# Where two columns of ones are filled: ahead of all loads, or behind the loads of chunk 2

## The chip, the cores and the metric

The kernel runs on one core of a Trainium2 chip. The metric is the device time of one execution in microseconds (us), median of three runs. A profile of one execution lies beside it; its rows count from the start of the profiled span.

## The reference

Two blocks follow one another. First comes a causal attention with 4 batches, 8 heads, 768 positions and 64 values per head. Heads 0, 2 and 6 see every earlier position ("retrieval"); the other five see the first 4 positions and a window of the last 64 ("streaming"). Its output, laid out as 3072 rows of 512, goes through two matrix products with a leaky ReLU between them:

```python
scores = scale * np.matmul(q, k.transpose(0, 1, 3, 2))
mask = np.where(retr[0, :, 0, 0, None, None], full_mask, stream_mask)
scores = np.where(mask[None, :, :, :], scores, -1000000000.0)
a = np.exp(scores - max)
a = a / (np.sum(a, axis=-1, keepdims=True) + 1e-09)
attn_out = np.matmul(a, v)
...
h = x @ w_in                    # 512 -> 2048
g = np.maximum(0.01 * h, h)
out = g @ w_out                 # 2048 -> 512
```

## The kernel before

The positions are cut into eight chunks of 384: chunks 0 and 1 are batch 0, chunks 2 and 3 batch 1, and so on. Each chunk goes through three stages: attention (class `Attention`, one unit for each streaming head and two to five for each retrieval head), the first product (`in_slots`, 16 ticks of four matmuls, L420) and the second product (`out_slots`, L433). TensorE (PE) does the scores (L302, L337, L282 for the first four positions, the "sinks"), the products with V (L271) and both MLP products. ScalarE (ACT) does the exponentials and the leaky ReLU, VectorE (DVE) the masks (L310, L312, L346), the division by the sum (L368, L370) and the copies out of the second product (L438).

The sum of a row of the softmax comes out of the product with V: each head's V has 65 columns, and the last is 1.0. V lies in two buffers, `va[0]` for the even batches and `va[1]` for the odd ones, each `[128, 6 blocks, 8 heads, 65]`. A load of V (`load_v`, L104) writes columns 0 to 63 of the three blocks of its chunk; column 64 is filled once per buffer, by a memset in `zero_small` (L159). `vb` holds the same V shifted by 64 positions, for the windows, and is copied out of `va` by `v_shift` (L132, L133). `zero_small` also zeroes `ksink` and `vs`, and `zero_keys` (L153, L154) zeroes the halves of the key buffer `kt` that no head fills.

The order is written by hand (`manual_schedule`): each engine takes its instructions in the order of the program, and a wait at one holds all behind it on that engine. The program text is, with the calls that matter here:

```python
zero_small(0, nc.vector)        # L476: va[0]'s ones
...
load_v(0, ...); load_qk(1); load_v(1)
load_in(...); load_out(...)     # both MLP matrices
load_qk(2)
load_v(2)                       # L498: into va[1], blocks 0 to 2
...                             # attention of chunk 0
zero_small(1, nc.vector)        # L555: va[1]'s ones
nc.vector.tensor_copy(vs[1][0:32, :, D], m_sink[0:32, :])
a1 = Attention(1, xt_eng="v").slots()
```

Loads from memory go through GpSimd's queue (POOL; `load_qk` L99, `load_v` L104, `load_in` L121, `load_out` L125). SyncE's queue (SP) carries the transposing copies of q and k (`turn_dma`, L210: `qb` to `qd` and `kb` to `kd`), `v_shift`, and the writes of the output (L439). Chunks 0 and 1 are transposed on TensorE, chunks 2 to 7 by those transposing copies; from `kd` DVE spreads the keys of each head into `kt` (`spreads`, L219).

After the attention of chunk 0 the order is: attention of chunk 1 mixed with the first product of chunk 0; the first product of chunk 1; seven slots (22 matmuls) of the second product of chunk 0; `spreads(2)`; the attention of chunk 2 mixed with what is left of the second products of chunks 0 and 1 and with `spreads(3)`; and then a loop over chunks 2 to 7 in which attention, first product and second product of neighbouring chunks are mixed slot by slot.

The buffers `kb` and `qb` are doubled: `load_qk(4)` waits for the transposing copies of chunk 2. `va[1]` takes chunks 2 and 3, then 6 and 7.

Of the kernel before, what the change touches and what calls it, by code (L numbers as in the profile page):

```python
# [21 lines left out]
def kernel(  # L22
# [12 lines left out]
    nc = tc.nc  # L35
    B, H, S, D = q.shape
# [21 lines left out]
    def bf(name, *shape):  # L58
        return one.tile([128, *shape], BF16, name=name)
# [14 lines left out]
    va = [bf(f"va{i}", 6, H, D + 1) for i in range(2)]  # L74
# [81 lines left out]
    def zero_small(i, eng):  # L156
        eng.memset(ksink[i][:], 0.0)
        eng.memset(vs[i][:], 0.0)
        eng.memset(va[i][:, :, :, D], 1.0)  # L159


    qx = {}
# [311 lines left out]
    load_sinks(0)  # L474
    zero_keys(0, nc.vector)
    zero_small(0, nc.vector)  # L476
    nc.vector.memset(shift[:], 0.0)
    for a in ats:
        nc.vector.memset(a[:, :, 1:3, :], 0.0)
    nc.gpsimd.memset(m_caus[:], 1.0)  # L480
# [72 lines left out]
    v_shift(1)  # L553
    zero_keys(1, nc.vector)
    zero_small(1, nc.vector)  # L555
    nc.vector.tensor_copy(vs[1][0:32, :, D], m_sink[0:32, :])

# [73 lines left out]
```

## Time and profile before

| | |
|---|---|
| device time, median of 3 | 276.74 us (276.65 to 277.5) |
| profiled execution, its own time | 275.88 us |
| its span (first to last instruction) | 274.2 us |
| mean granted TensorE clock | 0.944 of full speed |
| busy: PE, ACT, DVE, POOL | 229.7, 140.3, 95.5, 71.5 us |
| PE's share of the span | 84% |

The span is what the rows divide up; the 1.68 us between it and the execution's own time lie outside all rows. Busy shares are averages over the whole span, so a stretch in which an engine stands still is found in the slices and in the timelines. "Idle before" is the time that an engine stood still just ahead of an instruction, with the instruction or transfer that ended it.

### The profile page before, as it was taken

The page shows a single profiled execution, that of the slowest core. Times are in us where ns is not written, and L with a number is a line of the kernel's source. Part 1 is how long each engine was busy: PE and PEld are TensorE (multiplying, and loading weights), DVE is VectorE, ACT ScalarE, POOL GpSimd, SP SyncE. Part 2 cuts the span into 40 slices and gives each one's busy share as a digit, 9 for nine tenths or more (in the row PEclk, how much of TensorE's full clock was granted, in tenths as well). Part 3 has the DMA queues.
Part 4 walks back from the last instruction along what each step waited for, and adds up shares of the span by engine and source line. Part 5 has one row for each costly group of instructions (what it writes and reads, how often), then busy time and mean ns, then how long its engine had stood idle before and what let it go on. Part 6 is the DMA issues. An engine that isn't in the chain of part 4 may idle for free.

```text
span 274.2 us, 5026 instructions
## 1 busy us (share of the span) xinstructions
PE 229.7 (84%) x2036; PEld 138.0 (50%) x2036; DVE 95.5 (35%) x272; ACT 140.3 (51%) x305; POOL 71.5 (26%) x94
## 2 busy tenths in 40 slices
PE   1785000198999989999999999999999999999995
PEld 1463000066555555665565566656665566655544
DVE  7867100125200673265235315522353124311012
ACT  2859000067674455767565576565645766633300
POOL 8995135734700000399000007500000000000000
PEclk9979655589999999999999999999999999999999
DMA  7999999999990114599951088908210101010022
GB/s 82 131 138 201 214 206 166 148 126 165 190 105 2 44 54 108 107 146 155 185 153 39 2 186 89 167 7 175 75 41 4 37 38 41 0 41 38 38 79 77
DMA packets 98167, 27.40 MB, mean 100 GB/s; under 512 B 90464, under 2 KB 93792, under 8 KB 98144
## 3 DMA queue, kind: packets, MB, share of 16 engines
q0 software_dynamic: 74448, 13.64, 66.0%
q1 hardware_dynamic: 23696, 13.44, 21.1%
q8 instruction: 16, 0.26, 0.4%
q14 instruction: 7, 0.06, 0.1%
HBM read 27.30 MB, written 6.29 MB: 123 GB/s over the span
## 4 chain that ended last, share of the span: by engine, by line
PE 76%; DMA 11%; POOL 8%; DVE 2%; issue 1%; ACT 1%; DVEq 0%; POOLq 0%
PE ph L420 30%; PE py L433 27%; DMA w_out_bf<-in_moe_w_out_dram 8%; PE po L271 6%; PE psS L302 5%; PE psS L433 3%; DMA va<-in_v_dram 3%; POOL va L104 2%; PE psS L337 2%; PE psS L376 2%; PE psS L282 2%; POOL qb L99 1%; POOL kb L99 1%; DVE xs L370 1%; POOL w_in_bf L121 1%
## 5 line engine op out<-in xcount | busy, mean ns | idle before, releaser
L420 PE MATMUL ph<-xt,w_in_bf 128*128 128x384 bf16 x512 | 102.0, 327 | 0.0
L433 PE MATMUL py<-w_out_bf,g 128*128 128x512 bf16 (+1 forms) x352 | 91.4, 374 | 0.0
L422 ACT ACTIVATE g<-ph 128x384 bf16<-128x384 f32 x128 | 62.9, 491 | 54.7 <-PE ph L420 54.1
L420 PEld LDWEIGHTS <-w_in_bf 128*128 128x128 bf16 x512 | 46.0, 98 | 30.5 <-issue 1.9
L433 PEld LDWEIGHTS <-g 128*128 128x128 bf16 x400 | 35.8, 98 | 26.2
L307 ACT ACTIVATE at<-psS 128x384 bf16<-128x384 f32 x81 | 39.2, 489 | 14.0 <-PE psS L302 12.8
L271 PE MATMUL po<-va,at 128*128 128x65 bf16 x246 | 21.0, 196 | 27.2 <-DVE at L312 27.2
L271 PEld LDWEIGHTS <-at 128*128 128x128 bf16 x252 | 16.3, 100 | 33.1 <-DVE at L312 27.4
L438 DVE COPY o<-py 128x512 f32<-128x512 f32 (+1 forms) x22 | 14.9, 677 | 44.6 <-PE py L433 44.5
L104 POOL DMA_DIRECT2D va<-in_v_dram x24 | 21.4, 916 | 5.2 <-DMA w_out_bf<-in_moe_w_out_dram 3.4
L114 POOL TENSOR_TENSOR vs<-vsf,m_sink 32x448 bf16<-32x448 f32 x3 | 2.8, 941 | 75.6 <-PE psS L302 40.5
L99 POOL DMA_DIRECT2D kb<-in_k_dram x21 | 18.8, 905 | 13.8 <-DMA kd<-kb 8.6
L346 DVE TENSOR_TENSOR ats<-ats,m_win 128x384 bf16<-128x384 bf16 x40 | 14.3, 358 | 21.9 <-ACT ats L342 21.5
L302 PE MATMUL psS<-qd,kt 128*128 128x384 bf16 (+2 forms) x81 | 20.7, 290 | 0.2 <-ACT at L307 0.2
L342 ACT ACTIVATE ats<-psS 128x384 bf16<-128x384 f32 x38 | 18.4, 488 | 4.5 <-PE psS L337 4.5
L99 POOL DMA_DIRECT2D qb<-in_q_dram x21 | 18.5, 904 | 7.1 <-DMA w_in_bf<-in_moe_w_in_dram 3.8
L285 ACT ACTIVATE at_sink<-psS 128x384 bf16<-128x384 f32 (+1 forms) x7 | 3.1, 445 | 30.4 <-PE psS L282 30.3
L312 DVE TENSOR_TENSOR at<-at,m_caus 128x128 bf16<-128x128 bf16 x24 | 5.6, 232 | 33.1 <-ACT at L307 33.0
L370 DVE TENSOR_TENSOR xs<-po,linv 128x384 bf16<-128x384 f32 x30 | 16.7, 557 | 1.0
L378 ACT ACTIVATE xt<-psS 128x384 bf16<-128x384 bf16 x24 | 11.7, 489 | 7.9 <-PE psS L376 7.6
L302 PEld LDWEIGHTS <-kt 128*128 128x128 bf16 x108 | 10.4, 99 | 9.6 <-issue 3.2
L337 PEld LDWEIGHTS <-kt 128*128 128x128 bf16 x240 | 12.3, 99 | 5.6 <-issue 0.2
(89 smaller groups left out, 195.0 us busy)
## 6 DMA issues: line engine op xcount, KB each, us to landing
out_dram<-o SPq DMA_DIRECT2D x23, 256.0 KB, 2.2
va<-in_v_dram POOLq DMA_DIRECT2D x24, 128.0 KB, 6.1
kb<-in_k_dram POOLq DMA_DIRECT2D x21, 128.0 KB, 5.9
qb<-in_q_dram POOLq DMA_DIRECT2D x21, 128.0 KB, 5.9
w_out_bf<-in_moe_w_out_dram POOLq DMA_DIRECT2D x4, 512.0 KB, 19.6
vb<-va SPq DMA_DIRECT2D x8, 195.0 KB, 3.1
w_in_bf<-in_moe_w_in_dram POOLq DMA_DIRECT2D x2, 512.0 KB, 9.6
w_in_bf<-in_moe_w_in_dram POOLq DMA_DIRECT2D x1, 1024.0 KB, 15.2
```

The lines of the kernel that those rows point to most:

```text
L99: nc.gpsimd.dma_start(out=t[:, g], in_=nat[nm][b, c, :, :, g])
L104: nc.gpsimd.dma_start(out=va[b % 2][:, 3 * c + g, :, 0:D], in_=nat["v"][b, c, :, :, g])
L271: nc.tensor.matmul(o, lhsT=lhsT, rhs=rhs, start=first, stop=False, skip_group_check=True)
L302: nc.tensor.matmul(s[:, off : off + w], lhsT=kt[i][:, p, hh, 128 * kj : 128 * kj + 128], rhs=q_of(n, p, lo, CH), start=(j == 0), stop=(j = ...
L307: nc.scalar.activation(out=a[:, 0:off], in_=s[:, 0:off], func=ACTF.Exp, scale=SM)
L337: nc.tensor.matmul(s[:, 64 * m : 64 * m + 64], lhsT=kt[i][:, p, hh, k0 : k0 + 128], rhs=q_of(n, p, 64 * m, 64 * m + 64), start=(m == 0), s ...
L342: nc.scalar.activation(out=av_, in_=s[:, 0:CH].rearrange("p (j e f) -> p j e f", j=3, e=2), func=ACTF.Exp, scale=SM)
L370: nc.vector.tensor_tensor(xs[:], po[:, :, :, 0:D], linv.to_broadcast([128, 3, 2, D]), op=ALU.mult)
L420: nc.tensor.matmul(ph[:, 0:CH], lhsT=w_in_bf[:, g, 128 * t : 128 * t + 128], rhs=xts[n][:, g, :], start=(g == 0), stop=(g == KG - 1))
L422: nc.scalar.activation(out=gs[n][:, t, :], in_=ph[:, 0:CH], func=ACTF.Prelu, alpha=0.01)
L433: nc.tensor.matmul(py[n][:, 0 : c1 - c0], lhsT=gs[n][:, ng, 128 * tt : 128 * tt + 128], rhs=w_out_bf[:, ng, c0:c1], start=(ng == 0), stop= ...
L438: nc.vector.tensor_copy(o[:, 0 : c1 - c0], py[n][:, 0 : c1 - c0])
```

## The change

The memset of V's ones leaves `zero_small`, which is called once for each buffer (L476, L555). Both buffers are filled at the beginning instead, on the same engine, behind the memset of `shift` and ahead of those of `ats`; in the text of the program this stands ahead of every load of V.

```diff
     def zero_small(i, eng):
         eng.memset(ksink[i][:], 0.0)
         eng.memset(vs[i][:], 0.0)
-        eng.memset(va[i][:, :, :, D], 1.0)
...
     zero_small(0, nc.vector)
     nc.vector.memset(shift[:], 0.0)
+    for i in range(2):
+        nc.vector.memset(va[i][:, :, :, D], 1.0)
     for a in ats:
         nc.vector.memset(a[:, :, 1:3, :], 0.0)
```

## Rows read from the trace of the kernel before

**Rows 1.** Page, the span in 40 slices of 6.86 us: tenths busy, granted clock.

```profile
PE   1785000198999989999999999999999999999995
PEclk9979655589999999999999999999999999999999
```

**Rows 2.** Waits of 0 to 100 us: in total, times, longest.

```profile
PE po L271 <- DVE at L312: 27.2, 1, 27.2
POOL va L104 <- DVE va L159: 1.4, 1, 1.4
```

**Rows 3.** Timeline of DVE, 0 to 54 us: start, duration, instruction, idle before.

```profile
5.19 0.10 DVE L159 MEMSET va<- 128x48 bf16 x1
...
27.77 0.49 DVE L158 MEMSET vs<- 128x520 bf16 x1
53.09 0.10 DVE L159 MEMSET va<- 128x48 bf16 x1 [24.82 <-DMA va<-in_v_dram]
53.33 0.17 DVE L556 COPY vs<-m_sink 32x8 bf16<-32x8 bf16 x1
```

**Rows 4.** Chain that ended last, pieces of 0 to 110 us: start, us, what.

```profile
21.84 22.38 DMA w_out_bf<-in_moe_w_out_dram
...
45.79 6.97 DMA va<-in_v_dram
...
54.02 1.28 PE psS L282 x4
...
71.45 14.53 PE ph L420 x84
85.98 4.75 PE py L433 x22
```

**Rows 5.** Timeline of POOL, 0 to 75 us: issues of loads, their duration, idle before.

```profile
5.58 0.90 POOL L104 DMA_DIRECT2D va<-in_v_dram  x1
...
14.81 2.68 POOL L104 DMA_DIRECT2D va<-in_v_dram  x3
...
34.34 0.88 POOL L99 DMA_DIRECT2D qb<-in_q_dram  x1 [3.77 <-DMA w_in_bf<-in_moe_w_in_dram]
...
65.64 2.70 POOL L99 DMA_DIRECT2D kb<-in_k_dram  x3 [8.56 <-DMA kd<-kb]
```

**Rows 6.** PE's windows of 1 us: length, busy (instructions), granted clock, DMA share, GB/s.

```profile
29.00:30.00 1.00, 0.00 (x0) 1.00 1.17 219
30.00:31.00 1.00, 0.00 (x0) 0.58 1.09 207
...
56.00:57.00 1.00, 1.00 (x7) 0.50 3.19 164
```

**Rows 7.** Timeline of SP's queue, 20 to 110 us: issues of transfers.

```profile
52.30 4.43 SPq L210 DMA_TRANSPOSE kd<-kb  x1
...
65.27 3.59 SPq L210 DMA_TRANSPOSE kd<-kb  x1
...
69.59 0.54 SPq L133 DMA_DIRECT2D vb<-va  x1
```

**Rows 8.** Tile `kd`, the issue at 52.3 us: from issue to landing.

```profile
DMA to landing us min/median/max: 12.8/12.8/12.8
```

**Rows 9.** Tile `kd`, the issue at 65.3 us: from issue to landing.

```profile
DMA to landing us min/median/max: 9.7/9.7/9.7
```

**Rows 10.** Timeline of DVE, 88 to 104 us, where chunk 2's attention runs.

```profile
90.08 1.86 DVE L219 COPY kt<-kd 64x512 bf16<-64x512 bf16 x6
...
98.64 0.28 DVE L219 COPY kt<-kd 64x512 bf16<-64x512 bf16 x1
...
99.57 0.56 DVE L370 TENSOR_TENSOR xs<-po,linv 128x384 bf16<-128x384 f32 x1
```

**Rows 11.** Timeline of PE, 88 to 110 us.

```profile
100.44 0.33 PE L376 MATMUL psS<-ident,xs 128*128 128x128 bf16 x3
```

**Rows 12.** Page, DMA issues: count, KB each, us from issue to landing.

```profile
out_dram<-o SPq DMA_DIRECT2D x23, 256.0 KB, 2.2
```

## The prediction

> **What bounds the kernel now.** I read the page's slices first. TensorE is busy nearly everywhere from the ninth slice on, so that what is lost there is little; but in slices 5 to 7 (27 to 48 us) its digit is 0, and the granted clock falls to 5 tenths [rows 1]. So the question is what ends this hole. The list of waits names one: TensorE stood still for 27.2 us in one piece, until DVE's mask at L312 let the product with V go on [rows 2]. DVE's timeline says why the mask came so late: DVE was done with the memset of `vs` at 27.77 + 0.49 = 28.26, and then stood for 24.82 us at one memset of 0.10 us, L159 of `va[1]`, until a load of V had landed [rows 3]. The chain that ended last confirms the order: the second MLP matrix lands at 21.84 + 22.38 = 44.22, which lets POOL issue the rest of the loads; the last V of chunk 2 lands at 45.79 + 6.97 = 52.76; DVE wakes 0.33 us later; and TensorE goes on [rows 3, 4]. From there to the end the chain runs mostly on TensorE.
>
> The memset writes column 64 and the load writes columns 0 to 63, so no element is shared. Yet the memset stands behind the load in the program and waits for it, and with it waits everything that stands behind it on DVE: the copy into `vs`, the masks of chunk 1, and through them TensorE and ScalarE.
>
> **Removed: the wait.** Behind the memset of `vs`, which ends at 28.26, the next instruction is now the copy into `vs`. Between the end of L159 and that copy lay 53.33 - 53.19 = 0.14 us [rows 3], so I put the copy at 28.40 instead of 53.33: 24.93 us earlier. TensorE's pause shrinks from 27.2 to about 2.3 us. POOL's load of V of chunk 3 waited 1.4 us for the same memset [rows 2]; that goes too, but this load is needed only in chunk 3's attention, and the transposing copies behind which I queue below do not read it: 0.
>
> **Added: two memsets at the front.** L159 took 0.10 us at 5.19 [rows 3]; one of the two was there already, so DVE has 0.10 us more ahead of the copies of chunk 0's keys. POOL's first load of V, issued at 5.58 [rows 5], now waits for a memset that ends some 0.2 us later than 5.29, behind that of `shift`; that is still ahead of 5.58. Price between 0 and 0.1 us; I take 0, since the first stretch waits for loads and POOL rather than for DVE. The loads into `va[1]` wait for a memset long done: 0.
>
> **The clock.** TensorE had stopped at about 26.4 and kept full clock to 30; at 30 to 31 it fell, and when work came back it was still at 0.50 at 56 to 57 [rows 6]. A pause that ends at 28.7 ends before that fall, so I expect no half-clock piece. Four matmuls of 384 columns took 1.28 us at half clock (54.02) and take 14.53 / 84 x 4 = 0.69 at full clock [rows 4]; over the 3.8 us from 53.7 to about 57.5 half is some 1.9 us. Bounds: 0 if it falls all the same, 1.9 if not.
>
> **What is late next.** The work that moves forward meets transfers that do not. POOL's loads of chunk 2 wait for the MLP matrices (for instance 3.77 us at 34.34) and not for compute [rows 5], and SP's transposing copies wait for those loads, so both stay where they are. In order:
>
> The first product of chunks 0 and 1 and the second of chunk 0 need both matrices. The second matrix is there at 44.22 and is wanted at 85.98 - 24.93 = 61.05 [rows 4]; hidden.
>
> The keys of chunk 2: TensorE has its 22 matmuls of the second product done at 85.98 + 4.75 = 90.73 before, so at 65.8 after, or at 63.9 with the clock's gain [rows 4]. Then it needs `kt`, which DVE spreads from `kd`. That copy is issued at 52.30 and lands 12.8 later, at 65.1 [rows 7, 8]; POOL, which waited for the same copy, went on at 65.64 [rows 5], which agrees. With DVE's 0.33 us to wake, the spreading starts at 65.4 instead of 90.08 [rows 10]: 24.7 us earlier. So this landing swallows the clock's gain and 0.2 us besides. The forecast for this point is 24.7; TensorE should stand still for one to two us ahead of it.
>
> The keys of chunk 3: their first spreading stands at 98.64 [rows 10], which becomes 73.9. `kd` is issued at 65.27 and lands 9.7 later [rows 7, 9], at 74.97, so DVE can go on at 75.3 and stands for 1.4 us, with the masks and the division queued behind it. What TensorE waits for first is the division that ends at 99.57 + 0.56 = 100.13 [rows 10], wanted by the transposition at 100.44 [rows 11]: 0.3 us of slack. The loss is 1.4 - 0.3 = 1.1 us. Bounds: 0 if the masks behind it are absorbed by the product slots in between, 1.4 and the same again if the queue of DVE does not catch up, 2.7.
>
> Further on chunks 4 to 7 are loaded and transposed after work that itself moves forward, in the distance that they have now, and DMA is idle for long stretches there: 0.
>
> The sum: 24.7 - 1.1 = 23.6 us. On the profiled execution's own 275.88 this is 252.3. The median of the runs, 276.74, is 0.86 longer, and I forecast on it: 253.1 us.
>
> **A rule that speaks against it.** DVE now works while POOL issues chunk 2's loads, where it stood still before. The rows: three issues of V at 14.81, beside a busy DVE, took 2.68 / 3 = 0.89 us each; one with DVE standing took 0.88 [rows 5]. So the price is 0.01 us for each issue. The bound from rows, if POOL is held at each issue by one whole DVE instruction, the longest of the attention (0.56 us [rows 10]): four issues that chunk 2's transposing copies need are still to come after 28.4, the last of k and three of q, so 4 x 0.56 = 2.2 us if none of it vanishes in waits like the 3.77 us.
>
> The Trainium skill, page "SBUF — State Buffer", section "SBUF: two separate sides", says that while DVE runs an instruction in a mode that uses both ports, GpSimd can't write the descriptors of the transfers that its queue issues; it gives a transfer that takes about 620 ns alone and 3100 ns beside a DVE copy. By these figures four issues would lose some 4 x 2.5 = 10 us, an estimate, and the sum would be 263. The rows named above show no such stretching at a busy DVE, so I weigh it low.
>
> **Rivals.**
> 1. *The keys are not late.* If the copies land earlier than I place them, or the waits are absorbed, 24.9 us and the clock's 1.9 come through: 276.74 - 26.8 = 249.9; with the keys of chunk 2 as placed and those of chunk 3 absorbed, 252.0. For it: the landings were measured on queues in which some transfers now move. Against it: chunk 2's copy stands ahead of anything that moves.
> 2. *The keys of chunk 3 are later still.* The first writes of the output were ready long after these copies; now the first is ready at about 65 and waits in SP's queue behind the last copy of `vb` (69.59 + 0.54 [rows 7]). Two writes can then run beside the end of chunk 3's copy and the loads of chunk 4; at 2.2 us each [rows 12] the keys come up to 4.4 us later: up to 276.74 - 19.2 = 257.5. Against it: they stand behind the copy in SP's queue.
> 3. *POOL is held by DVE*, as above: 253.1 + 2.2 = 255.3.
> 4. *The wait moves on to another instruction* of DVE that needs the same load. The copy into `vs` and the masks of chunk 1 read nothing of chunk 2, so I see none: 276.7.
> 5. *Slower.* Without the long pause TensorE gets half clock on, from 28.7 us: what it does from 71.45 to 85.98 would then take twice its 14.53 us. This costs the whole gain once more than 23.6 us of full-speed work ran at half clock. Against it: before, full clock came back soon after a pause of 27 us [rows 2, 6].
>
> **How the numbers follow.** My sum, at 252.0 to 254.7 by the bounds of chunk 3's wait: 60%. Rival 1, 249.5 to 252.0: 14%. Rival 2, 254.7 to 257.5: 18%. Rival 3: 4%. Rivals 4 and 5: 2% each. The predicted time is 253.1, the range 250.5 to 257.0, which leaves out the ends of rivals 1 and 2 and all of 4 and 5. A measurement can tell about 0.3% of the time, 0.8 us, from no change: faster 96%, same 2%, slower 2%.
>
> **What would show it.** DVE goes from the memset of `vs` to the copy within 0.3 us; the hole of [rows 1] is gone, and the granted clock stays near full from 20 us on; L307 and L312 of chunk 1 run on through 28 to 45; SP's copies of chunk 2 are issued where they were; DVE waits for `kd` ahead of L219 twice, at about 65 and 74. Wrong would be: a wait of TensorE on DVE of more than 5 us before 60; transposing copies issued later than 53 us; POOL's issues of q stretched above 1 us; or, past 80 us, distances between the chunks that are not those of before.

## The result, and the profile after

The changed kernel takes 253.58 us (median; 253.04 to 253.69) against 276.69 for the kernel before, a ratio of 0.9156 with a 95% interval of 0.9133 to 0.9178. That is 23.1 us less; the forecast was 23.6 less, and 253.1. The profiled execution took 253.04 with a span of 251.3, which is 22.9 below the span before. A second set of runs of the same kernel gave 252.97 (0.9167, 0.9139 to 0.9196). Three later executions, of 256.77, 278.58 and 1327.54 us, ran slow; the ratios leave them out, and they shift the medians below by less than 0.2 us.

The slices of the page of the changed kernel, of 6.28 us each, answer to [rows 1]:

```profile
PE   1975698999888999999999999999999999999994
PEclk9999989999999999999999999999999999999999
```

The hole is gone. What is left of it lies in the fifth slice, the 6 (25.1 to 31.4 us); the 5 ahead of it stands in [rows 1] too. The waits of 0 to 100 us (in total, times, longest) show what became of the two lines of [rows 2], and one line that is new:

```profile
PE po L270 <- DVE at L311: 2.2, 1, 2.2
...
DVE kt L218 <- DMA kd<-kb: 1.3, 1, 1.3
```

TensorE's wait for DVE's mask fell from 27.2 to 2.2 us. DVE waits once for the transposed keys, 1.3 us. POOL's wait for the memset of `va[1]` is not in the list any more. DVE's timeline, beside [rows 3] and [rows 10]:

```profile
28.28 0.49 DVE L158 MEMSET vs<- 128x520 bf16 x1
28.80 0.17 DVE L557 COPY vs<-m_sink 32x8 bf16<-32x8 bf16 x1
...
64.80 0.69 DVE L437 COPY o<-py 128x512 f32<-128x512 f32 x1 [17.62 <-PE py L432]
65.58 2.44 DVE L218 COPY kt<-kd 64x512 bf16<-64x512 bf16 x6
...
76.26 0.29 DVE L218 COPY kt<-kd 64x512 bf16<-64x512 bf16 x1 [1.29 <-DMA kd<-kb]
```

From the memset of `vs` DVE goes straight to the copy. It reaches the keys of chunk 2 as they land, and those of chunk 3 1.29 us ahead of their landing. SP's queue, beside [rows 7], and the landings of its two copies, beside [rows 8, 9]:

```profile
52.42 5.27 SPq L209 DMA_TRANSPOSE kd<-kb  x1
...
64.45 5.42 SPq L209 DMA_TRANSPOSE kd<-kb  x1
```

```profile
DMA to landing us min/median/max: 13.1/13.1/13.1
```

```profile
DMA to landing us min/median/max: 11.8/11.8/11.8
```

So the keys land at 65.5 and 76.25, against 65.1 and 74.97 before. The transfers stand nearly where they stood, and the work has moved up to them.

Where the 22.9 us come from is read off TensorE's timeline. The main marks are the beginning of the second product and chunk 2's last transposition of attention; between them stands a product with V of chunk 2 (L271, L270 in the changed kernel). In the kernel before they are at

```profile
85.82 4.91 PE L433 MATMUL py<-w_out_bf,g 128*128 128x512 bf16 x22
...
92.59 0.27 PE L271 MATMUL po<-va,at 128*128 128x65 bf16 x3
...
105.47 0.34 PE L376 MATMUL psS<-ident,xs 128*128 128x128 bf16 x3
```

and in the changed kernel at

```profile
61.14 4.91 PE L432 MATMUL py<-w_out_bf,g 128*128 128x512 bf16 x22
...
67.48 0.23 PE L301 MATMUL psS<-qd,kt 128*128 128x128 bf16 x1 [0.46 <-DVE kt L218]
...
68.85 0.27 PE L270 MATMUL po<-va,at 128*128 128x65 bf16 x3 [0.32 <-DVE at L309]
...
77.56 0.34 PE L375 MATMUL psS<-ident,xs 128*128 128x128 bf16 x3 [0.71 <-DVE xs L369]
...
82.61 0.34 PE L375 MATMUL psS<-ident,xs 128*128 128x128 bf16 x3
```

The first mark is 85.82 - 61.14 = 24.7 us earlier, the last 105.47 - 82.61 = 22.9; and 22.9 is also what the span has lost. So 1.8 us are given back between the two, within chunk 2's attention, and nothing behind it. Half of it is gone by the product with V, which is 92.59 - 68.85 = 23.7 us earlier, behind waits for DVE's spreading copies and masks; the other half goes at the transposition that waits for the division, 100.44 [rows 11] against 77.56, 22.9 earlier. From that last transposition to the end of the span it is 168.7 us in both.

### The profile page after: what moved, and what is told of

It is laid out like the page before. It is cut to its first block, busy times and chain, and to the rows that moved or that the text cites. A ratio compares the mean times of both kernels' runs of the same rounds, so it can differ in the third digit from the quotient of the medians.

```text
span 251.3 us, 5025 instructions
## 1 busy us (share of the span) xinstructions
PE 230.8 (92%) x2036; PEld 138.3 (55%) x2036; DVE 96.9 (39%) x272; ACT 140.3 (56%) x305; POOL 71.4 (28%) x94
## 4 chain that ended last, share of the span: by engine, by line
PE 73%; DMA 11%; DVE 6%; POOL 5%; ACT 2%; issue 2%
PE ph L419 28%; PE py L432 25%; PE po L270 6%; DMA kd<-kb 5%; PE psS L301 5%; DMA va<-in_v_dram 4%; PE psS L432 3%; DMA qb<-in_q_dram 2%; PE psS L375 2%; PE psS L336 2%; POOL qb L99 2%; POOL va L104 2%; PE psS L281 1%; DVE kt L154 1%; DVE kt L153 1%
## 5 line engine op out<-in xcount | busy, mean ns | idle before, releaser
L270 PE MATMUL po<-va,at 128*128 128x65 bf16 x246 | 20.8, 195 | 2.5 <-DVE at L311 2.2
L270 PEld LDWEIGHTS <-at 128*128 128x128 bf16 x252 | 16.2, 99 | 8.4 <-DVE at L311 2.3
L377 ACT ACTIVATE xt<-psS 128x384 bf16<-128x384 bf16 x24 | 11.7, 488 | 8.8 <-PE psS L375 8.5
L270 PEld LDWEIGHTS <-ats 128*128 128x128 bf16 x240 | 11.8, 99 | 4.6 <-DVE ats L345 0.8
```

The costliest lines, as they stand in the source:

```text
L270: nc.tensor.matmul(o, lhsT=lhsT, rhs=rhs, start=first, stop=False, skip_group_check=True)
```

## The experiments

Each kernel was timed beside the kernel before. The baseline changed a little from one set to the next (275.6 to 276.7), so times are compared within a set where less than 1 us matters. The changed kernel was timed again in one later set only; the first four experiments are set against it by their ratios to the kernel before.

**The load behind the memset.** The kernel before, with one line moved:

```diff
     load_qk(2)
-    load_v(2)
...
     zero_small(1, nc.vector)
+    load_v(2)
     nc.vector.tensor_copy(vs[1][0:32, :, D], m_sink[0:32, :])
```

> The kernel before, its memset of the ones of va[1] left where it was, but the loads of V of chunk 2 written behind it in the program; POOL reaches them as late as before. If the cost was nothing but the order of memset and load (my theory), DVE no longer stops at the memset, and the time is that of the changed kernel, 253.6, or up to 0.5 us less, since nothing is added at the front. Rival: what counts is that the memset left its old place, or that it runs at the start; then the time stays near 276.7.

Measured: 252.79 us, 0.915 (0.9113 to 0.9188). The memset stays where it was and costs nothing there; what cost was that it stood behind the load of the same buffer in the program. DVE's rows at that place:

```profile
28.16 0.49 DVE L158 MEMSET vs<- 128x520 bf16 x1
...
28.77 0.10 DVE L159 MEMSET va<- 128x48 bf16 x1
```

The same memset of 0.10 us, without the 24.82 us of idle time ahead of it. That the whole gain comes without touching the front also says that the front of the changed kernel neither earns nor costs much.

**The ones on POOL.** The kernel before, with the memset of `va[1]`'s ones at its old place on POOL:

```diff
-        eng.memset(va[i][:, :, :, D], 1.0)
+        (nc.gpsimd if i else eng).memset(va[i][:, :, :, D], 1.0)
```

> The kernel before, with the memset of the ones of va[1] at its old place in the program but on POOL instead of DVE. DVE is free as in the changed kernel, and the wait for the V of chunk 2 now holds POOL's queue, so that the loads of q and k of chunk 3 are issued near 53 us instead of 46. Theory that the transposed keys of chunk 3 come next: they land some 6 us later than 76.2, TensorE waits for them, and the time is 253.6 + 5 to 6.5, so 258.5 to 260. Rival: the keys of chunk 3 have slack or the masks behind them are absorbed; 253.6 to 255. Rival: the wait costs wherever it stands; 270 or more.

Measured: 254.24 us, 0.9199 (0.9164 to 0.9234). The wait for the same load now stands on POOL. The median is 0.7 us above that of the changed kernel, not the 5 to 6.5 that I had expected, and the intervals of the two ratios overlap, so that no cost is shown. POOL stands 6.06 us at the memset and issues the loads of chunk 3 from 53.31; but the transposing copy of chunk 2's keys, which takes 13.1 us in the changed kernel, now takes 4.1:

```profile
52.79 0.31 POOL L159 MEMSET va<- 128x48 bf16 x1 [6.06 <-DMA va<-in_v_dram]
53.31 2.62 POOL L99 DMA_DIRECT2D kb<-in_k_dram  x3 [0.21 <-issue]
```

```profile
DMA to landing us min/median/max: 4.1/4.1/4.1
```

```profile
77.09 0.29 DVE L219 COPY kt<-kd 64x512 bf16<-64x512 bf16 x1 [2.31 <-DMA kd<-kb]
```

The loads of chunk 3 were issued 7 us later and yet its keys came only 0.8 us later (77.09 against 76.26). My step from "issued later" to "lands later by as much" was wrong: while the copy of chunk 2 and the loads of chunk 3 run together they hold each other up. Chunk 3's loads of q took a median of 10.2 us from issue to landing in the changed kernel, and 5.5 here.

**Late zeros.** The changed kernel, with the remaining memsets ahead of chunk 1's attention moved behind it:

```diff
-    zero_keys(1, nc.vector)
-    zero_small(1, nc.vector)
-    nc.vector.tensor_copy(vs[1][0:32, :, D], m_sink[0:32, :])
     a1 = Attention(1, xt_eng="v").slots()
...
     turn_dma(2)
     v_shift(2)
     load_qk(3)
     load_v(3)
+    zero_keys(1, nc.vector)
+    zero_small(1, nc.vector)
+    nc.vector.tensor_copy(vs[1][0:32, :, D], m_sink[0:32, :])
     run(in_slots(1, ("ph",)))
```

> The changed kernel, with the memsets of kt[1], ksink[1] and vs[1] and the copy into vs moved from ahead of the attention of chunk 1 to behind it, where DVE stands idle for some 17 us. This takes away the 2.2 us for which TensorE still waits for DVE near 29 us, and with it the half-clock stretch near 31 to 34 us if the pause is what brings it. TensorE then reaches the attention of chunk 2 some 3 to 3.5 us sooner. Theory that the transposed keys of chunks 2 and 3 end what is won: they land where they did, and the time is 253.6 less 0 to 0.6. Rival: TensorE's own work decides; 253.6 - 3 = 250.5.

Measured: 253.09 us, 0.9155 (0.9117 to 0.9192), no different from the changed kernel. TensorE does begin the second product 2.5 us earlier (58.62 against 61.14), and the granted clock stays at 1.00 through 30 to 34 us, where it fell in the changed kernel. All of it ends in one wait of DVE:

```profile
65.61 2.44 DVE L218 COPY kt<-kd 64x512 bf16<-64x512 bf16 x6 [2.64 <-DMA kd<-kb]
```

The spreading starts at 65.61 as it did at 65.58. So the landing of chunk 2's keys is a floor, as the prediction had it, and the changed kernel stands just on it.

**Chunk 2's loads ahead of the second MLP matrix**, with late zeros:

```diff
+    load_qk(2)
+    load_v(2)
     for i in range(4):
         load_out(i)
-    load_qk(2)
-    load_v(2)
```

> As the run with late zeros, and the loads of q, k and V of chunk 2 issued ahead of the second MLP matrix instead of behind it. The keys of chunk 2 then land some 10 us earlier than 65.5, so they no longer decide; the loads of chunk 3 stand behind the same bytes as before, so their keys land near 76 still or a little earlier. Theory that keys decide, chunk by chunk: the wait moves to the keys of chunk 3 alone, and 0.5 to 1.5 us come through against the run with late zeros: 251.5 to 253. Rival, TensorE's own work decides: no difference between the two runs. Second rival: the second MLP matrix becomes late at about 58 us; the time is longer than with late zeros alone.

Measured: 258.15 us, 0.9329 (0.9298 to 0.936): 5 us slower than with late zeros alone, so the expectation failed, and not by the second rival: TensorE begins the second product at 59.38 without a wait for the matrix. Chunk 2's keys land at 60.5, 5 us earlier, and DVE does not wait for them. Chunk 3's keys come later: their copy is issued at 67.59 instead of 65.00 and takes 11.7 us instead of 9.1. POOL stood 3.45 us for the matrix ahead of its last load of q of chunk 3, so the matrix's bytes, which now travel beside chunk 3's loads, are the likely cause; this was not tried apart.

```profile
79.35 0.28 DVE L218 COPY kt<-kd 64x512 bf16<-64x512 bf16 x1 [6.08 <-DMA kd<-kb]
```

```profile
80.66 0.50 PE L375 MATMUL psS<-ident,xs 128*128 128x128 bf16 x3 [5.50 <-DVE xs L369]
```

DVE stands 6.08 us at the spreading of chunk 3's keys, and TensorE 5.50 at the transposition that waits for the division queued behind it: the very step by which the prediction priced chunk 3's keys, with a larger wait. This transposition is 3.7 us later than with late zeros (77.00 there), but the last one of the chunk 5.9 us (87.96 against 82.04): during the standstill the granted clock fell, and TensorE did its next work at half clock. Its windows of 1 us (length, busy (instructions), granted clock, DMA share, GB/s):

```profile
79.00:80.00 1.00, 0.00 (x0) 0.50 1.10 207
...
84.00:85.00 1.00, 1.00 (x4) 0.50 0.05 16
```

**One raw buffer.** Next I let POOL's loads wait until the copies have landed, by taking away the second buffer; and, with it as the measure, the changed kernel again:

```diff
-            t = rot.tile([128, 3, H, D], BF16, name=f"{nm}b", tag=f"{nm}b", bufs=2)
+            t = rot.tile([128, 3, H, D], BF16, name=f"{nm}b", tag=f"{nm}b", bufs=1)
```

> The changed kernel itself, unaltered, as the measure for the three others on the same chip: 253.0 to 253.9.

Measured: 252.97 us. In the traced execution (253.56 us) DVE waits for neither copy: TensorE begins the second product at 62.40 instead of 61.14 and reaches chunk 2 a little later than the keys. The landing of the keys and TensorE's own arrival lie so near each other that either can come last.

> The changed kernel, with one buffer instead of two for the raw q and k of a chunk, so that POOL's loads of the next chunk wait until the transposing copies of this one have landed. In the run with the ones on POOL the copy of chunk 2's keys took 4.1 us instead of 13.1 while POOL's loads paused. Theory that the loads and the transposing copies share the DMA engines and that this sets when the keys land: keys of chunk 2 near 56 us, of chunk 3 near 68, no wait of DVE for either, and 1 to 2 us less than the changed kernel: 251.5 to 252.5. Rival: the queues are better kept full; the keys of chunk 3 come later than 76 and the time is 255 or more.

Measured: 252.10 us, 0.9117 (0.9096 to 0.9139). A second set of runs, for its trace:

> The changed kernel with one buffer for raw q and k once more, for its trace. By its times (251.6 to 252.2) I expect the keys of chunk 2 to have landed near 56 and those of chunk 3 near 72, no wait of DVE for either, and the six spreading copies of chunk 2 within 1.9 us or beside POOL's issues within 2.9.

Measured: 251.80 us, 0.9125 (0.9089 to 0.9162). The two copies of SP's queue and their landings:

```profile
53.15 1.90 SPq L209 DMA_TRANSPOSE kd<-kb  x1
...
70.25 2.35 SPq L209 DMA_TRANSPOSE kd<-kb  x1
```

```profile
DMA to landing us min/median/max: 4.0/4.0/4.0
...
DMA to landing us min/median/max: 4.1/4.1/4.1
```

Each copy takes 4 us instead of 13.1 and 11.8, and the keys are there at 57.2 and 74.35, although the loads of chunk 3 were issued 11 us later than in the changed kernel. Against the changed kernel in the first of the two sets the time falls by 0.9 us, and the intervals meet at 0.9139, so the gain is at the edge of what the runs can tell. A new wait shows that the single buffer has a price further on: DVE stands 2.50 us for chunk 4's keys, at 93.85. It is small: from chunk 2's last transposition (81.21) to the end of the span (250.1) it is 168.9 us instead of 168.7.

**Three raw buffers**, the other way:

```diff
-            t = rot.tile([128, 3, H, D], BF16, name=f"{nm}b", tag=f"{nm}b", bufs=2)
+            t = rot.tile([128, 3, H, D], BF16, name=f"{nm}b", tag=f"{nm}b", bufs=3)
```

> The changed kernel, with three buffers instead of two for raw q and k, so that POOL issues the loads of chunk 4 from about 56 us on, beside the transposing copy of chunk 2, instead of waiting for its landing at 65.5. Two questions. First, the loads share the DMA engines with the transposing copies: then chunk 2's keys land later than 65.5 or chunk 3's later than 76, and the time is 254 to 257; rival, that fuller queues help, 252.5 or less. Second, POOL has then issued everything before DVE spreads chunk 2's keys: if POOL's issuing is what slows those six copies from 1.86 us to 2.4 to 2.9, they take 1.9 us again; if it is the traffic itself, they stay at 2.4 or more.

Measured: 257.10 us, 0.9348 (0.9298 to 0.9397); of the four executions the one with the trace was the shortest, at 255.62. In it POOL issues chunk 4's keys at 56.96 instead of 66.09, and chunk 3's keys land later:

```profile
78.87 0.29 DVE L218 COPY kt<-kd 64x512 bf16<-64x512 bf16 x1 [2.79 <-DMA kd<-kb]
```

The first question is answered: with one, two and three buffers the times are 252, 253 to 253.6 and 257. The second was not tried as I had meant it: POOL was still issuing q of chunk 4 at 66.53, beside the first of the six spreading copies, which took 2.29 us. The rows of the single copies settle it all the same; they stand in the last section.

**Mended front**, and mended front with late zeros and one buffer:

```diff
     zero_small(0, nc.vector)
+    nc.vector.memset(va[0][:, :, :, D], 1.0)
     nc.vector.memset(shift[:], 0.0)
-    for i in range(2):
-        nc.vector.memset(va[i][:, :, :, D], 1.0)
...
     load_qk(2)
+    nc.vector.memset(va[1][:, :, :, D], 1.0)
     load_v(2)
```

> The changed kernel, with the ones of va[0] ahead of the memset of shift, as before, and those of va[1] behind the memsets of ats, right ahead of the loads of V of chunk 2 in the program. POOL's first load of V then no longer waits 0.15 us for DVE. Theory that this wait, and nothing else at the front, costs: 0.1 to 0.5 us less than the changed kernel, or nothing where the transposed keys decide (they hang on POOL's queue, so they may come 0.15 us sooner). Rival: the run with the loads behind the memset was 0.8 us ahead because of its front; then 0.6 to 1.0 less.

Measured: 252.68 us, 0.915 (0.9128 to 0.9172), against 252.97 for the changed kernel in the same set: the intervals overlap, so nothing is shown but that it is small. POOL's first load of V went from 5.73 back to 5.59.

> One buffer for raw q and k, the memsets of kt[1], ksink[1] and vs[1] behind the attention of chunk 1, and the mended front together. With two buffers the late memsets won 0.5 us or less, since DVE then waited 2.6 us for the keys of chunk 2. Theory: with keys in time the 3 us of the late memsets come through; 248.5 to 250. Rival: something else than the keys swallows them (the second MLP product, ScalarE); 251.5 to 252.5, as the run with one buffer alone.

Measured: 250.85 us, 0.9076 (0.905 to 0.9103), 2.1 below the changed kernel in its set, and the intervals lie apart. The late zeros alone gave nothing that could be measured; with keys in time they and the mended front give 1.2 us on top of the one buffer, and 1.6 in the next set. In both sets the intervals of the two kernels overlap, so that this gain is likely and not shown. DVE waits for no key; TensorE's only wait of a microsecond near 30 us is now another:

```profile
30.04 0.19 PE L270 MATMUL po<-vb,ats 128*128 128x65 bf16 x1 [1.64 <-DMA vb<-va]
```

This is the shifted V of chunk 1. The second set of the same kernel served as measure for one more:

> The kernel of one raw buffer, late memsets and mended front once more, as the measure for the next: 249.7 to 251.4.

Measured: 250.20 us, 0.907 (0.9033 to 0.9107), the fastest version of the study.

**V of chunk 3 first**, on top of it:

```diff
-    load_qk(3)
     load_v(3)
+    load_qk(3)
```

> As the run before it, with V of chunk 3 loaded ahead of q and k of chunk 3, so that POOL's three issues of it fall near 49 us instead of 63 to 65.7, where DVE spreads the keys of chunk 2. In the traces so far six spreading copies took 1.86 us with POOL standing and 2.4 to 2.9 with POOL issuing. Theory that POOL's issues slow DVE's copies and that this stretch is on the path: the six take near 1.9 us and the time falls by 0.5 to 1.0, to 249.9 to 250.4. Rival: the slow copies are off the path; no difference. Second rival: V now runs beside the transposing copy of chunk 2's keys, which lands later; slower.

Measured: 250.73 us, 0.9099 (0.907 to 0.9128): no difference. It didn't test what it was meant to: POOL then issued q of chunk 3 in that stretch instead of V, and the six copies took 3.06 us. The copy of chunk 2's keys, beside the three loads of V, took 6.8 us instead of 4.2, as the second rival had it; the keys were there at 58.5, before DVE wanted them.

```profile
63.29 3.06 DVE L218 COPY kt<-kd 64x512 bf16<-64x512 bf16 x6
```

**Six of the kernels together.** The last transposition of chunk 2's attention on TensorE, against the span of the same execution:

| kernel | transposition, us | span, us | difference |
|---|---|---|---|
| before | 105.47 | 274.2 | 168.7 |
| changed | 82.61 | 251.3 | 168.7 |
| late zeros | 82.04 | 250.7 | 168.7 |
| loads ahead of the matrix | 87.96 | 256.6 | 168.6 |
| three buffers | 85.22 | 253.9 | 168.7 |
| one buffer, late zeros, front | 80.19 | 248.9 | 168.7 |

Whatever these six do ahead of this point, the rest takes 168.6 or 168.7 us.

## Why the prediction was right, point by point

**The removed wait**: forecast 24.93 us earlier, the copy into `vs` at 28.40. It stands at 28.80, so 24.53. The 0.4 us are in the front: DVE begins to zero `kt[1]` at 24.91 instead of 24.41. Is this the price of the added memsets? POOL's first load of V did wait for them:

```profile
5.73 0.90 POOL L104 DMA_DIRECT2D va<-in_v_dram  x1 [0.15 <-DVE va L478]
```

This wait I had excluded by a margin of some 0.1 us, and it is there. But the zeroing begins at 24.80 and 24.86 in two kernels whose POOL issues that load at 5.59 and 5.58 without a wait, and at 24.30 with the mended front. So the front differs by half a microsecond from execution to execution, and no more than the 0.15 can be put down to the memsets.

**The clock** was the wrong step. I argued that a pause that ends at 28.7 ends before the fall. TensorE went on at 29.15, and the granted clock fell all the same, in the stretch where it had fallen before, and came back within 33 to 34 us. Its windows of 1 us (length, busy, granted clock, DMA share, GB/s), beside [rows 6]:

```profile
29.00:30.00 1.00, 0.85 (x11) 1.00 1.14 223
30.00:31.00 1.00, 1.00 (x8) 0.60 1.11 209
31.00:32.00 1.00, 1.00 (x9) 0.50 1.16 219
...
33.00:34.00 1.00, 1.00 (x9) 0.69 1.29 222
34.00:35.00 1.00, 1.00 (x11) 1.00 1.20 197
```

So a half-clock stretch (1.2 of 2.4 GHz) of some 3.4 us remains where before there was one of 3.8, and the 1.9 us shrink to little: the second product begins 24.7 us earlier where the copy into `vs` stands 24.5 earlier. In the second trace of the changed kernel the stretch was longer:

```profile
28.00:29.00 1.00, 0.00 (x0) 0.62 1.12 231
...
34.00:35.00 1.00, 1.00 (x7) 0.50 1.23 198
```

This is most of why TensorE began the second product 1.3 us later there. The three other executions of the first set, at 253.5 to 253.7 us, were granted 0.980 of full speed on the mean, and the traced one, at 253.04, 0.993. With late zeros, where TensorE paused 1.41 us instead of 2.22, the fall did not come. The pause alone does not decide, though: with one raw buffer the clock fell while TensorE was still busy, ahead of a pause of 1.81 us that ended at 28.86:

```profile
24.00:25.00 1.00, 0.64 (x2) 0.86 1.12 182
25.00:26.00 1.00, 0.98 (x8) 0.50 1.18 193
```

What brings the fall in this stretch stays open. The forecast didn't suffer, since by its own next step the keys would have taken the gain. But that the second product comes 24.7 us earlier, the number that the forecast had from the landing of the keys, is luck: here it comes from work that arrived without the clock's gain.

**Chunk 2's keys**: forecast landing at 65.1 and spreading from 65.4; measured 65.5 and 65.58. The expected standstill of TensorE ahead of it did not come, because without the clock's gain TensorE arrives only then. The late zeros supplied the gain, and with it the standstill, 2.64 us on DVE: that the landing is a floor is shown.

**Chunk 3's keys**: forecast that DVE waits 1.4 us and goes on at 75.3; measured 1.29 us and 76.26. The mechanism is as forecast, down to the transposition that waits for the division (77.56, 0.71 us idle); TensorE loses 0.9 us there, where 1.1 were forecast. That the wait is so near is luck in part, since its two ends moved together: DVE came to it at 74.97 instead of 73.9, and the keys landed at 76.25 instead of 74.97. They were later because the copy took 11.8 us and not 9.7; in the other execution of the same kernel it took 8.5 and there was no wait. So its duration varies by some 3 us between executions, with the loads beside it.

**A term that was missing**: the six spreading copies of chunk 2 took 2.44 us instead of 1.86, 0.6 us more, and the five copies into `ksink` behind them 0.82 instead of 0.56. The landing that lets DVE spread also lets POOL issue the loads of chunk 4, so that the two now fall together; in the kernel before, POOL had nothing to do at that point:

```profile
66.09 2.71 POOL L99 DMA_DIRECT2D kb<-in_k_dram  x3 [9.97 <-DMA kd<-kb]
```

The sum, at the marks of TensorE: 24.7 at the second product, less 1.8 in chunk 2's attention, where the forecast had 24.7 less 1.1. Chunk 3's keys took 0.9 of the 1.8, near the forecast's 1.1; the other 0.9 went at the spreading, where the sum had nothing. That is the term that was missing, and it makes up the difference of 0.7.

**Past chunk 2**: forecast 0, measured 0 (the table).

**The rivals.** That the keys are not late (1) holds in some executions, as the second trace of the changed kernel shows, but there because TensorE came later, with more half clock; the gain that the rival forecast did not come. That writes of the output push chunk 3's keys by up to 4.4 us (2): the first write was issued at 71.23, behind the copies of `vb`, and the keys were 1.3 us later than forecast; whether by the writes was not tried apart. That POOL is held by DVE (3): the four issues for chunk 2 took 0.87 us each, as with DVE standing, the last of them beside DVE's division at 39.04:

```profile
33.99 0.87 POOL L99 DMA_DIRECT2D qb<-in_q_dram  x1 [3.83 <-DMA w_in_bf<-in_moe_w_in_dram]
...
39.12 0.87 POOL L99 DMA_DIRECT2D qb<-in_q_dram  x1 [1.73 <-DMA w_out_bf<-in_moe_w_out_dram]
```

The Trainium skill, page "SBUF — State Buffer", section "SBUF: two separate sides", has GpSimd kept from writing the descriptors of its transfers while DVE runs in a two-port mode; by its figures (some 620 ns alone, 3100 beside a copy) the issues would have stretched to some 3 us, an estimate. Here they did not, but no row says whether the division runs in such a mode, so this is no test of the rule. Of the other two rivals nothing showed: DVE waits for no V of chunk 2, and the clock is full from 34 us on.

## What to carry to other kernels

An instruction that needs nothing can still be made to wait by the order of the program, if it touches the same buffer as a transfer written ahead of it; look for the wait of a very short instruction that ends with a transfer, and write it ahead of the transfer. To price its removal, follow the transfers that do not move with it, and ask for each when the work will meet it: here 22.9 of 24.9 us came through, and half of the loss was not a late transfer but the work that its landing set off on POOL. And a transfer that is late was helped less here by an earlier issue than by fewer others beside it: of the three ways to reorder loads only the one that let POOL wait made the kernel faster, by 0.9 us.

## What the runs showed of the hardware that I had not expected

A transposing copy from SP's queue of the keys of chunk 2 or 3 took 4.0 to 4.2 us when POOL's loads stood still or were issued only from its middle on, 6.8 beside three loads of V, and 8.5 to 15.3 us beside the loads of a chunk.

DVE's spreading copies of 64 x 512 elements take 0.28 to 0.29 us each with POOL standing, and often twice that or more beside POOL's work. The clearest rows are those of the kernel with three raw buffers. POOL's issues there, and the six copies of chunk 2, of which the first runs beside the one issue and the last beside the other:

```profile
66.53 0.88 POOL L99 DMA_DIRECT2D qb<-in_q_dram  x1 [1.81 <-DMA va<-in_v_dram]
68.73 2.63 POOL L104 DMA_DIRECT2D va<-in_v_dram  x3 [1.32 <-DMA va<-in_v_dram]
```

```profile
66.79 0.70 DVE L218 COPY kt<-kd 64x512 bf16<-64x512 bf16 x1
67.52 1.55 DVE L218 COPY kt<-kd 64x512 bf16<-64x512 bf16 x5
```

The windows of the first copy and of the next two (length, busy (copies that touch the window), granted clock, DMA share, GB/s) show the same traffic beside both:

```profile
66.79:67.49 0.70, 0.70 (x1) 1.00 2.89 145
67.52:68.12 0.60, 0.57 (x2) 1.00 2.88 151
```

So it is not the traffic that slows them, but what POOL itself does. The 14 traces of the study hold 504 such copies. The 245 during which POOL ran nothing took 0.275 to 0.293 us; of the 259 that overlap an instruction of POOL 125 took more than 0.35, up to 1.04. Which part of POOL's work holds a copy is not shown, since about as many beside it stay quick. The Trainium skill, page "SBUF — State Buffer", section "SBUF: two separate sides", says that of GpSimd and a DVE instruction in a two-port mode whichever starts first gets the ports that they share and the other blocks; these rows agree, if the copies run in such a mode, which no row tells, and have DVE be the one that is held.

TensorE's clock fell after a pause of 2.2 us that had already ended, while TensorE was busy for 0.85 and more of each microsecond; in another trace, shown above, it fell ahead of the pause.
